# A block-sparse attention with a token and a channel mixer: four chunk pairs by seven block products and one plain chunk, in place of three pairs and three plain chunks

## Chip, cores, metric

One core of a Trainium2 chip. The metric is device time in microseconds of one execution, the median of the runs. Engines are named as in the profile: PE is TensorE, DVE VectorE, ACT ScalarE, POOL GpSimd, SP SyncE.

## What is computed

```python
scores = q @ k.T / sqrt(64), rel = i - j kept where 0 <= rel < 64     # batch 8, heads 8, seq 576, head_dim 64
x = softmax(scores) @ v                          # as (8, 576, 512)
h = relu(x^T @ w_tok1) @ w_tok2                  # 576 -> 256 -> 576 over tokens
u = x + h^T
out = u + relu(u @ w_ch1) @ w_ch2                # 512 -> 1536 -> 512 over channels
```

Weights come as 64-bit floats and are turned into 32-bit ones on the chip. All large products use a pair (hi, lo) for each operand: hi is the operand rounded by a cast, lo the rest, and three matmuls (hi x hi, hi x lo, lo x hi) make one product.

## The kernel before, in words

**Attention** (lines 481 to 594, passes i = -1 to 36). 36 tiles of 128 query rows; each pass works on several tiles at once. In pass i TensorE transposes the exponentials of tile i (`pp`, L312), runs a piece of the second token product (`up`, L413 and L420), the first token product of earlier tiles (`h`, L372), the value product (`xp`, L324), the scores of tile i+2 (`s`, L282) and a second piece of `up`. ScalarE copies `pp` to `pt` (L314), casts a weight piece (`w1hi`, L109), makes eight exponentials per tile in two groups of four (L305), each followed by a reading of the sum, copies `up` to `u` between the groups (L425), casts `xhi` (L109) and copies the second piece of `up`. VectorE makes the masked scores (L297), a reciprocal, the steps of a weight conversion (L204 to L219), and the scaling of `xp` to `x` (L341). GpSimd makes `xlo` (L112), the last add of a conversion (`w`, L221) and `w1lo`. `up` has one PSUM buffer until pass 35. Every engine works through its queue in the order in which the program issues.

**Jobs.** The weights' conversion is cut into 39 jobs of up to 384 columns (0 to 3 and 4 to 6 the token weights, 7 to 22 the first channel weight, 23 to 38 the second). `JOBS` says how many a pass takes; `N_FIRST` = 28 are done in the attention, the other 11 in plain chunk 0.

**Channel mixer.** The 4608 tokens are nine chunks of 512. A *plain* chunk is 144 matmuls into `gp` (`gemm1`, L635), a relu with split (L622, L623), and 144 into `op` (`gemm2`, L643). A *pair* of chunks takes both as the columns of a 2 x 2 block matrix and needs seven block products in place of eight (`first_product`, L913, `second_product`, L969): 12 units of 42 matmuls, 504 in place of 576. The weights' block sums m1 to m7 that pairs need are in DRAM (`w1s`, `w2s`); `load_unit` brings one unit's into a ring of three slots three units ahead. Chunks 0, 1 and 2 are plain (`N_PLAIN` = 3), and three pairs follow. While chunks 1 and 2 run, `weight_steps` forms the sums on VectorE and ScalarE, 128 x 256 at a time, and SyncE stores them; in chunk 2 the first pair's token blocks are combined (`sums`, `prep`).

Of the kernel before, what the change touches and what calls it, by code (L numbers as in the profile page):

```python
# [3 lines left out]

# [17 lines left out]
C = H * D  # L22
# [17 lines left out]
N_FIRST = 28  # L40


JOBS = {i: 1 if 0 <= i < 5 or i in (7, 8, 12, 18, 27) or i > 8 and i % TPP not in (0, 3, 5) else 0 for i in range(-1, 37)}
# [10 lines left out]
N_PLAIN = 3  # L54
# [4 lines left out]
HOME = {"m1": "c2", "m6": "c3", "m7": "c4", "m5": "c5", "m2": "c6", "m4": "c0", "m3": "c1"}  # L59
# [6 lines left out]
STEPS_FT = {1: (2, 2, 2, 2, 1, 0, 2, 2, 0, 1, 1, 0), 2: (2, 1, 0, 1, 1, 0, 0, 0, 0, 0, 0, 0)}  # L66
STEPS_CT = {1: (2, 2), 2: (3, 0)}
# [23 lines left out]
def mixer_kernel(ctx: ExitStack, tc: tile.TileContext, qh, kh, vh, wt1, wt2, wc1, wc2, out):  # L91
# [11 lines left out]
    w1s = [dram.tile([P, NH, NPROD, 2, P], F32, name=f"w1s{k}") for k in range(2)]  # L103
    w2s = [dram.tile([P, NG, 2, NPROD, 2, P], F32, name=f"w2s{k}") for k in range(2)]
# [26 lines left out]
    with ExitStack() as actx:  # L131
# [6 lines left out]
        kbs, loaded, cpool = {}, {}, [pq]  # L138
# [47 lines left out]
        abs_of = {}  # L186

        def job_abs():
            if to_convert:
                n, raw = to_convert[0]  # L190
                m = jobs[n][4]
                abs_of[n] = cpool[0].tile([P, CW], I32, name=f"c{n}", tag="cvc", bufs=2)[:, :m]
                high = raw[:, :m].bitcast(F32).rearrange("p (n t) -> p n t", t=2)[:, :, 1]
                nc.scalar.activation(abs_of[n].bitcast(F32), high, AF.Abs)

        def to_f32_a(raw, n, tag, late=False):
# [3 lines left out]
            if late:  # L200
                c = abs_of.pop(tag)
            else:
                c = cpool[0].tile([P, CW], I32, name=f"c{tag}", tag="cvc", bufs=2)[:, :n]
                nc.vector.tensor_scalar(out=c, in0=high, scalar1=0x7FFFFFFF, scalar2=None, op0=ALU.bitwise_and)  # L204
# [4 lines left out]
            return c, low, high, n, tag, late  # L209

        def to_f32_b(c, low, high, n, tag, late):

            r = cpool[0].tile([P, CW], I32, name=f"r{tag}", tag="cvr", bufs=1)[:, :n]
            w = cpool[0].tile([P, CW], F32, name=f"w{tag}", tag="cvw", bufs=2)[:, :n]
# [6 lines left out]
            (nc.vector if late else nc.gpsimd).tensor_add(w, rf, cf)  # L221
# [5 lines left out]
        jobs += [(wc1, w1hi, w1lo, o, CW) for o in range(0, NCT * F, CW)]  # L227
# [3 lines left out]
        def job_load():  # L231
            if to_load:
                n = to_load.pop(0)
                src, _, _, o, m = jobs[n]
                raw = cpool[0].tile([P, CW], I64, name=f"raw{n}", tag="raw", bufs=3)
                nc.sync.dma_start(raw[:, :m], src[:, o:o + m])
                to_convert.append((n, raw))
# [3 lines left out]
        def job_convert_a():  # L241
            if to_convert:
                n, raw = to_convert.pop(0)
                to_convert_b.append((n, to_f32_a(raw, jobs[n][4], n, n >= N_FIRST)))

# [7 lines left out]
        def job_finish():  # L253
            if to_finish:
# [5 lines left out]
                else:  # L260
                    eng = nc.vector if src is wt2 or n >= N_FIRST else nc.gpsimd
                    split(nc.scalar, eng, hi[:, o:o + m], lo[:, o:o + m], w)
                    if src is wt1 and o + m == 5 * DT:
                        for c, r in enumerate((top, bottom)):
                            nc.gpsimd.tensor_copy(t1z[r, c], t1lo[r, 4 * DT:].bitcast(F32))

# [216 lines left out]
        for i in range(-1, NT + 1):  # L483
# [63 lines left out]
            while to_load and len(to_convert) < 2 and i < NT - 2:  # L547
                job_load()
            if i == NT - 1:
                while to_convert or to_convert_b or to_finish:  # L550
                    job_convert_a()
                    job_convert_b()
                    job_finish()
                qctx.close()
                pu = uctx.enter_context(tc.tile_pool(name="pu", bufs=1, side="right", reuse_waits="tile"))
                ul = {0: load_u(0, pu)}
        for ct in range(NCT):
# [4 lines left out]
    with ExitStack() as bctx:  # L562
# [15 lines left out]
        cpool[0] = pl  # L578
        first = [(o, min(C, jobs[N_FIRST][3] - o)) for o in range(0, jobs[N_FIRST][3], C)]
        w2_raw = []  # L580

        def load_w2():
            if first:
                o, m = first.pop(0)
                raw = pl.tile([P, C], F32, name=f"raww2_{o}", tag="raww2", bufs=2)
                nc.sync.dma_start(raw[:, :m], w2_dram[:, o:o + m])
                w2_raw.append((o, m, raw))

        def split_w2():
            if w2_raw:  # L590
                o, m, raw = w2_raw.pop(0)
                split(nc.scalar, nc.vector, w2hf[:, o:o + m], w2lf[:, o:o + m], raw[:, :m])

        to_load += range(N_FIRST, len(jobs))
        for n in to_load:
            jobs[n] = (wc2, w2hf, w2lf) + jobs[n][3:]
        for _ in range(3):
            job_load()

        def late_steps():  # L600

            job_abs()
            yield
            while to_convert or to_convert_b or to_finish:
                job_convert_a()
                if to_load:
                    job_load()
                yield
                job_finish()
                yield  # L610
                job_convert_b()
                job_abs()
                yield

        late = late_steps()

        def w1_at(ft, ct):
            o = (ft // NH * NCT + ct) * NH * P + ft % NH * P
            return slice(o, o + P)

# [18 lines left out]
        def gemm2(op, ct, fts, gs, first, last, cols=slice(0, CHUNK)):  # L639
            k = 0  # L640
            for ft, (ghi, glo) in zip(fts, gs):
                for w, x in ((w2hi, ghi), (w2hi, glo), (w2lo, ghi)):
                    nc.tensor.matmul(op, w[:, ct, ft], x[:, cols], start=(first and k == 0),  # L643
# [15 lines left out]
        def store_w1(m, k, f0, ct, src):  # L659
# [434 lines left out]
```

## Time and profile before

| | |
|---|---|
| time, median of 3 runs | 805.61 us (805.21 to 806.02) |
| profiled execution | 806.01 us, its span 804.1 us |
| granted TensorE clock | 0.999 |
| attention, to the first `gp` matmul | 255.8 us |
| plain chunks 0, 1, 2 | 66.5, 65.3, 67.0 us |
| three pairs, to the last matmul | 345 us |
| DMA traffic | 180.59 MB, mean 225 GB/s |

Times in the timeline are us from the span's start. A row there gives start, length, engine, line, operation, tiles, and in brackets how long the engine stood idle before it and for whom. Matmuls are pipelined: a 512-column matmul is listed with 0.39 us, but starts follow each other closer. In the windows view, columns are the window, its length, busy time and count of PE, PEld, DVE, ACT and POOL, then the clock, the DMA share and GB/s.

### The profile page before, as it was taken

Reading aid. Unit: us, or ns where it says so; the run is one execution under the profiler, and the core shown is the slowest. Engines: PE = TensorE matmul, PEld = TensorE weight load, DVE = VectorE, ACT = ScalarE, POOL = GpSimd, SP = SyncE. Lnnn points to the kernel's source line nnn. Section 1 sums busy time; section 2 is a strip of 40 time slices with the busy share of each in tenths; the row PEclk is TensorE's granted clock in tenths of the full one; section 3 lists DMA queues with packets and bytes.
Section 4 is the critical chain, followed back from the end, with each engine's and each line's share of the span. In section 5 each row is a group of like instructions: output and inputs, shape, how many; then the busy total and the mean of one; then the engine's idle time right before and its main releaser. Section 6 shows DMA issues by size and latency. Waiting matters only on the chain. (4 is left out here: it accounts for less than half of the span.)

```text
span 804.1 us, 15810 instructions
## 1 busy us (share of the span) xinstructions
PE 789.7 (98%) x5749; PEld 655.2 (81%) x5749; DVE 567.8 (71%) x1529; ACT 388.4 (48%) x1124; POOL 265.1 (33%) x241
## 2 busy tenths in 40 slices
PE   8999999999999999999999999999999999999997
PEld 6667888888889878888878888888888888888886
DVE  5978789589572895777787474756666666656576
ACT  6998889889874440323334141326332244324040
POOL 3634544445330000000000050549832648723140
PEclk9999999999999999999999999999999999999999
DMA  9856778768635637877555775764985755965543
GB/s 352 274 183 227 231 252 302 236 211 297 218 113 169 198 102 213 255 227 236 196 170 179 281 287 183 246 239 170 315 327 206 287 187 166 364 228 190 199 161 104
DMA packets 86828, 180.59 MB, mean 225 GB/s; under 512 B 8800, under 2 KB 51808, under 8 KB 84832
## 3 DMA queue, kind: packets, MB, share of 16 engines
q1 hardware_dynamic: 84640, 177.76, 64.1%
q10 hardware_dynamic: 2112, 1.84, 0.7%
q8 instruction: 45, 0.74, 0.4%
q14 instruction: 31, 0.25, 0.1%
HBM read 137.69 MB, written 41.88 MB: 223 GB/s over the span
## 5 line engine op out<-in xcount | busy, mean ns | idle before, releaser
L913 PE MATMUL gp<-m,w1hi 128*128 128x512 f32 x504 | 155.8, 390 | 0.4 <-POOL m L794 0.4
L112 POOL TENSOR_TENSOR m7lo<-t3g,m7hi 128x512 fp32r<-128x512 f32 x18 | 23.4, 1302 | 359.5 <-ACT m7hi L109 359.5
L305 ACT ACTIVATE e<-e,nm 128x128 f32<-128x128 f32 x288 | 112.3, 399 | 6.1 <-DVE nm L297 6.1
L913 PEld LDWEIGHTS gp<-m,w1hi 128*128 128x128 f32 x504 | 94.7, 188 | 20.9 <-POOL m L794 1.3
L913 PE MATMUL gp<-m,w1lo 128*128 128x512 f32 x252 | 98.2, 389 | 0.0
L958 DVE TENSOR_TENSOR uf<-op,uf 128x512 f32<-128x512 f32 (+1 forms) x91 | 61.9, 684 | 40.5 <-PE op L969 30.7
L297 DVE CUSTOM_DVE_ANT_0 e<-s,mask 128x128 f32<-128x128 f32 x288 | 63.5, 286 | 12.2 <-PE s L282 12.1
L305 ACT ACTIVATION_READ_ACCUMULATOR e<-e,nm 128x1 f32 x288 | 56.5, 196 | 0.0
L112 POOL TENSOR_TENSOR xlo<-x,xhi 128x512 fp32r<-128x512 f32 x32 | 41.2, 1287 | 46.0 <-ACT xhi L109 45.7
L635 PE MATMUL gp<-uhi,w1hi 128*128 128x512 f32 x144 | 56.1, 389 | 0.0
L635 PE MATMUL gp<-ulo,w1hi 128*128 128x512 f32 x144 | 56.1, 389 | 0.0
L635 PE MATMUL gp<-uhi,w1lo 128*128 128x512 f32 x144 | 56.1, 389 | 0.0
L913 PEld LDWEIGHTS gp<-m,w1lo 128*128 128x128 f32 x252 | 47.3, 188 | 9.7
L643 PE MATMUL op<-ghi,w2hi 128*128 128x512 f32 x128 | 50.0, 390 | 0.9 <-ACT ghi L622 0.9
L643 PE MATMUL op<-glo,w2hi 128*128 128x512 f32 x128 | 50.0, 390 | 0.2 <-DVE glo L623 0.2
L643 PE MATMUL op<-ghi,w2lo 128*128 128x512 f32 x128 | 49.9, 389 | 0.0
L916 ACT COPY x<-gp 128x512 f32<-128x512 f32 x18 | 10.6, 587 | 81.2 <-PE gp L913 81.2
L221 POOL TENSOR_TENSOR w<-r,c 128x384 f32<-128x384 f32 (+1 forms) x28 | 27.6, 985 | 60.5 <-DVE r L219 58.5
L324 PEld LDWEIGHTS xp<-v,pt 128*64 128x64 f32 x1152 | 36.6, 138 | 12.9 <-ACT e L305 10.1
L341 DVE TENSOR_TENSOR x<-xp,ri 128x512 f32<-128x512 f32 x36 | 24.8, 690 | 30.3 <-PE xp L324 29.7
L312 PE MATMUL pp<-ident,e 128*128 128x128 f32 x288 | 44.6, 281 | 1.4
L420 PE MATMUL up<-t2hi,hhi 128*128 128x320 f32 (+1 forms) x128 | 43.0, 336 | 0.0
(204 smaller groups left out, 2042.4 us busy)
## 6 DMA issues: line engine op xcount, KB each, us to landing
v<-vh SPq DMA_DIRECT2D x36, 512.0 KB, 3.8
w1hi<-w1s SPq DMA_DIRECT2D x18, 896.0 KB, 4.9
w1lo<-w1s SPq DMA_DIRECT2D x18, 896.0 KB, 6.9
w1hi<-w2s SPq DMA_DIRECT2D x18, 896.0 KB, 4.6
w1lo<-w2s SPq DMA_DIRECT2D x18, 896.0 KB, 6.4
raw<-wc SPq DMA_DIRECT2D x32, 384.0 KB, 4.4
q<-qh SPq DMA_DIRECT2D x36, 256.0 KB, 4.9
k<-kh SPq DMA_DIRECT2D x7, 1280.0 KB, 8.3
```

The costliest lines, as they stand in the source:

```text
L112: eng_lo.tensor_sub(lo, src, hi.bitcast(F32))
L221: (nc.vector if late else nc.gpsimd).tensor_add(w, rf, cf)
L297: nc.vector.tensor_tensor_reduce(out=e[:, h], in0=s[:, h], in1=mk, scale=-scale, scalar=MAX_F32, op0=ALU.add, op1=ALU.min, accum_out=nm[:, ...
L305: nc.scalar.activation(e[:, h], e[:, h], AF.Exp, bias=nm[:, g:g + 1], scale=-1.0, accum_out=sm[:, g:g + 1])
L312: nc.tensor.transpose(pp[:, h], e[:, h], ident)
L324: nc.tensor.matmul(xp[half * BLK:(half + 1) * BLK, h], pts[h % 2][:, h // 2, half * BLK:(half + 1) * BLK], vt[:, half, h], start=True, sto ...
L341: nc.vector.tensor_mul(x, xp, ri.unsqueeze(2).to_broadcast([P, H, D]))
L420: nc.tensor.matmul(up[:, :n], hx[:, cs], w[:, tt * S + s0:tt * S + s0 + n], start=False, stop=(k == 6), skip_group_check=True)
L635: nc.tensor.matmul(gp, w[:, w1_at(ft, ct)], x[:, ct], start=(k == 0), stop=(k == 3 * NCT - 1))
L643: nc.tensor.matmul(op, w[:, ct, ft], x[:, cols], start=(first and k == 0), stop=(last and k == 3 * len(gs) - 1), skip_group_check=not (fir ...
L913: nc.tensor.matmul(b[INTO[m]], w[:, at], c[:, h, t], start=(k < 4 and z == y == 0), stop=(z == 1 and y == 2), skip_group_check=True)
L958: eng.tensor_add(x, y, x)
```

## The change

`N_PLAIN` is 1: chunk 0 alone is plain, and eight chunks make four pairs.

- 35 of the 39 conversion jobs now lie in the attention (`JOBS`: one more in passes 21, 30, 32 and two in passes 31, 33, 34 and 35); the last four run in chunk 0 (`tail_job`), through `w2_dram`.
- The first channel weight's sums are formed in the attention, passes 15 to 34 (`sums1_steps`). One block goes through five steps: VectorE adds hi and lo back together; GpSimd makes four sums; ScalarE casts the first row's hi and issues its store; GpSimd makes its lo, ScalarE casts the second row's hi and issues its store; GpSimd makes that lo. The lo stores are issued by ScalarE at the next step. `shi`, the cast's tile, has one buffer. Raw blocks are stored by SyncE (`RAW1`).
- The second weight's sums: two of six blocks in chunk 0, four in the first pair (`SUMS2`), GpSimd and ScalarE again. The first pair's token blocks are combined in chunk 0.

```diff
-N_FIRST = 28
+N_FIRST = 35
-N_PLAIN = 3
+N_PLAIN = 1
+SUMS1 = {i: (1, 0) for i in (15, 17, 18, 21, 25, 28)}
+SUMS1.update({i: (1, 1) for i in (16, 19, 20, 22, 24, 26, 27, 29, 30, 31, 33, 34)})
...
+        def store_sums():
+            for to, t in sum_stores:
+                nc.scalar.dma_start(to.rearrange("p m x -> p (m x)"), t.bitcast(F32))
+            sum_stores.clear()
+
+        def sum_steps(whole, buffers, negate, target, one_row):
+
+            w = buffers(None)
+            whole(w)
+            yield
+            (a11, a12), (a21, a22) = ([x[:, c * WW:(c + 1) * WW] for c in range(2)] for x in w)
+            nc.gpsimd.tensor_add(a22, a22, a21)
+            nc.gpsimd.tensor_sub(a21, a11, a21)
+            nc.gpsimd.tensor_sub(a11, a22, a11)
+            nc.gpsimd.tensor_sub(a12, a12, a11)
+            yield
+            for rows in ((0,), (1,)) if one_row else ((0, 1),):
+                his = [buffers(r) for r in rows]
+                for r, hi in zip(rows, his):
+                    if negate and r == 1:
+                        nc.scalar.mul(a22, a22, -1.0)
+                    nc.scalar.copy(hi, w[r])
+                    nc.scalar.dma_start(target(0, 2 + 2 * r).rearrange("p m x -> p (m x)"), hi.bitcast(F32))
+                yield
+                for r, hi in zip(rows, his):
+                    lo = w[r].bitcast(F32R)
+                    nc.gpsimd.tensor_sub(lo, w[r], hi.bitcast(F32))
+                    sum_stores.append((target(1, 2 + 2 * r), lo))
+                if rows[-1] == 1 or not one_row:
+                    yield
...
+                    return pq.tile([P, C], F32R, name=f"shi{f}_{r}", tag="shi", bufs=1)
...
             if i >= N_START:
                 for _ in range(n_jobs):
                     job_convert_b()
+            sums1_steps(SUMS1.get(i, (0, 0))[0])
+            for _ in range(RAW1.get(i, 0)):
+                next(raw1_left)
...
+            sums1_steps(SUMS1.get(i, (0, 0))[1])
```

ScalarE's queue in pass 20, before, from one `pt` to the next (the digits behind a name are the tile's or job's number and a buffer number):

```order
L314 COPY pt20_1_2502<-pp20_1_2497 128x512
L109 CAST w1hi_66<-w15_2425 128x384
L305 ACTIVATE e21_0_2506,sum21_2505<-e21_0_2506,nm21_2504 128x128 x4
L425 COPY u2_1_2481<-up2_1_1_2525 128x320
L305 ACTIVATE e21_1_2511,sum21_2505<-e21_1_2511,nm21_2504 128x128 x4
L109 CAST xhi20_2593<-x20_2573 128x512
L425 COPY u2_1_2481<-up2_1_2_2597 128x320
L314 COPY pt21_0_2619<-pp21_0_2614 128x512
```

The same place now, `shi1_0` and `shi1_1` being the two rows' casts of block 1 and `w1s0` the DRAM tensor that takes them:

```order
L390 COPY pt20_1_2528<-pp20_1_2523 128x512
L115 CAST w1hi_66<-w15_2442 128x384
L381 ACTIVATE e21_0_2532,sum21_2531<-e21_0_2532,nm21_2530 128x128 x4
L501 COPY u2_1_2503<-up2_1_1_2551 128x320
L381 ACTIVATE e21_1_2537,sum21_2531<-e21_1_2537,nm21_2530 128x128 x4
L298 CAST shi1_0_2582<-sw1_0_2448 128x512
L299 DMA w1s0_69<-shi1_0_2582 128x512
L115 CAST xhi20_2622<-x20_2602 128x512
L501 COPY u2_1_2503<-up2_1_2_2626 128x320
L298 CAST shi1_1_2640<-sw1_1_2449 128x512
L299 DMA w1s0_69<-shi1_1_2640 128x512
L390 COPY pt21_0_2652<-pp21_0_2647 128x512
```

Two casts and two stores stand between the exponentials and the next `pt`. GpSimd's queue at the same place, before:

```order
L112 TENSOR_TENSOR w1lo_67<-w15_2425,w1hi_66 128x384
L221 TENSOR_TENSOR w16_2551<-r16_2550,c16_2536 128x384
L112 TENSOR_TENSOR xlo20_2594<-x20_2573,xhi20_2593 128x512
L112 TENSOR_TENSOR w1lo_67<-w16_2551,w1hi_66 128x384
L112 TENSOR_TENSOR xlo21_2708<-x21_2687,xhi21_2707 128x512
```

And now, L303 being the low part of a block's row, which reads `shi`:

```order
L118 TENSOR_TENSOR w1lo_67<-w15_2442,w1hi_66 128x384
L216 TENSOR_TENSOR w16_2577<-r16_2576,c16_2562 128x384
L118 TENSOR_TENSOR xlo20_2623<-x20_2602,xhi20_2622 128x512
L303 TENSOR_TENSOR sw1_0_2448<-sw1_0_2448,shi1_0_2582 128x512
L118 TENSOR_TENSOR w1lo_67<-w16_2577,w1hi_66 128x384
L216 TENSOR_TENSOR w17_2708<-r17_2707,c17_2693 128x384
L303 TENSOR_TENSOR sw1_1_2449<-sw1_1_2449,shi1_1_2640 128x512
```

The first row's low part stands behind `xlo20`, the second's behind `w17`. GpSimd's queue in passes 32 to 34, before:

```order
L112 TENSOR_TENSOR xlo32_4067<-x32_4042,xhi32_4066 128x512
L221 TENSOR_TENSOR w25_4137<-r25_4136,c25_4116 128x384
L112 TENSOR_TENSOR xlo33_4180<-x33_4159,xhi33_4179 128x512
L221 TENSOR_TENSOR w26_4257<-r26_4256,c26_4242 128x384
L112 TENSOR_TENSOR xlo34_4282<-x34_4279,xhi34_4281 128x512
```

And now, with block 5's four sums (L288 to L291):

```order
L118 TENSOR_TENSOR xlo32_4220<-x32_4195,xhi32_4219 128x512
L216 TENSOR_TENSOR w29_4297<-r29_4296,c29_4272 128x384
L216 TENSOR_TENSOR w30_4303<-r30_4302,c30_4276 128x384
L288 TENSOR_TENSOR sw5_1_4099<-sw5_1_4099 128x256
L289 TENSOR_TENSOR sw5_1_4099<-sw5_0_4098,sw5_1_4099 128x256
L290 TENSOR_TENSOR sw5_0_4098<-sw5_1_4099,sw5_0_4098 128x256
L291 TENSOR_TENSOR sw5_0_4098<-sw5_0_4098 128x256
L118 TENSOR_TENSOR xlo33_4352<-x33_4331,xhi33_4351 128x512
L216 TENSOR_TENSOR w31_4439<-r31_4438,c31_4420 128x384
L216 TENSOR_TENSOR w32_4445<-r32_4444,c32_4424 128x384
L303 TENSOR_TENSOR sw5_0_4098<-sw5_0_4098,shi5_0_4370 128x512
L118 TENSOR_TENSOR xlo34_4476<-x34_4473,xhi34_4475 128x512
```

The four sums stand behind the adds of two jobs (`w29`, `w30`), and the low part behind two more.

More of the change, by code (lines that the diff above doesn't have):

```diff
@@ L753, in load_unit, with sums2, whole @@
+        def sums2(n, buffers):
+            g, t = divmod(n, 2)
+            def whole(w):
+                for row in range(2):
+                    o = ((2 * row + t) * NFT + 4 * g) * P
+                    nc.sync.dma_start(w[row], w2_dram[:, o:o + 2 * WW])
+            return sum_steps(whole, buffers, True, lambda k, at: w2s[k][:, g, t, at:at + 2], False)
         def load_unit(n):
```

394 lines of the change are left out of this document (187 added, 207 removed).

## The prediction

> **What bounds the kernel now.** I read the page first, then TensorE's timeline at the stage borders, then the chain of waits.
>
> ```profile
> span 804.1 us, 15810 instructions
> ...
> PE 789.7 (98%) x5749; PEld 655.2 (81%) x5749; DVE 567.8 (71%) x1529; ACT 388.4 (48%) x1124; POOL 265.1 (33%) x241
> ...
> ACT  6998889889874440323334141326332244324040
> POOL 3634544445330000000000050549832648723140
> ```
> TensorE is busy throughout. ScalarE is at eight or nine tenths in the first third, which is the attention, and at a third after it.
>
> ```profile
> 255.82 0.39 PE L635 MATMUL gp<-uhi,w1hi 128*128 128x512 f32 x1
> ...
> 322.30 0.39 PE L635 MATMUL gp<-uhi,w1hi 128*128 128x512 f32 x1
> ...
> 454.57 0.62 PE L913 MATMUL gp<-m,w1hi 128*128 128x512 f32 x2
> ```
> These rows of the timeline are the first matmuls of plain chunk 0, of plain chunk 1, and of the first pair. So the attention takes 255.8 us, plain chunk 0 66.5, and plain chunks 1 and 2 together 132.27.
>
> ```profile
> 531.10 19.05 PE gp L913 x84
> ...
> 761.37 19.04 PE gp L913 x84
> ```
> In the chain, the same place of the first and of the third pair lies 230.27 us apart: one pair takes 115.13 us, borders included. From 19.04 us for 84 matmuls, a 512-column matmul takes 0.2267 us. Plain chunks and pairs are TensorE's, with hardly a wait.
>
> In the attention, one tile as an example (tile 25), ScalarE and then TensorE:
>
> ```profile
> 170.85 1.07 ACT L314 COPY pt<-pp 128x512 f32<-128x512 f32 x2
> ...
> 175.25 0.39 ACT L305 ACTIVATE e<-e,nm 128x128 f32<-128x128 f32 x1
> ...
> 175.64 0.62 ACT L109 CAST xhi<-x 128x512 fp32r<-128x512 f32 x1
> 177.02 0.37 ACT L425 COPY u<-up 128x256 f32<-128x256 f32 x1 [0.77 <-PE up L420]
> 177.51 1.07 ACT L314 COPY pt<-pp 128x512 f32<-128x512 f32 x2
> ```
> ```profile
> 175.83 0.44 PE L413 MATMUL up<-ident,x 128*128 128x128 f32 x2
> ...
> 176.82 1.03 PE L312 MATMUL pp<-ident,e 128*128 128x128 f32 x8
> 177.69 0.38 PE L413 MATMUL up<-ident,x 128*128 128x128 f32 x2
> ...
> 180.11 1.15 PE L324 MATMUL xp<-v,pt 128*64 128x64 f32 x32
> 181.19 1.10 PE L282 MATMUL s<-k,q 64*64 64x128 f32 x32
> 182.23 0.44 PE L413 MATMUL up<-ident,x 128*128 128x128 f32 x2
> ```
> A tile takes 6.66 us (170.85 to 177.51). TensorE issues without a pause; ScalarE has 0.77 us to spare, just ahead of its second copy of `up`. TensorE needs that copy at 177.69 and `pt` at 180.11: a ScalarE that is late by more than these margins stops it, since `up` has one buffer.
>
> **The change part by part.** The sum is made against the profiled execution, 806.0 us (span 804.1), 0.4 above the median of the runs, 805.6.
>
> *Matmuls.* A pair has 504 matmuls, two plain chunks 576. Plain chunks 1 and 2 go (132.27 us) and a fourth pair comes (115.13): **-17.1 us**. Of that 72 x 0.2267 = 16.3 is arithmetic; the rest is a wait of plain chunk 2, less a pair's border. If the new chunk 0 has that wait too, it is 16.3: small.
>
> *Weight sums in the attention.* For each of six blocks VectorE adds hi and lo twice (512 columns, 0.69 us as in the row below), GpSimd makes four sums of 256 columns and two low parts, and ScalarE makes two casts and issues four stores.
>
> ```profile
> 234.49 0.69 DVE L341 TENSOR_TENSOR x<-xp,ri 128x512 f32<-128x512 f32 x1 [0.89 <-PE xp L324]
> ...
> L221 POOL TENSOR_TENSOR w<-r,c 128x384 f32<-128x384 f32 x17 | 17.1, 1003 | 35.0 <-DVE r L219 33.0 <-issue 2.0
> L112 POOL TENSOR_TENSOR xlo<-x,xhi 128x512 fp32r<-128x512 f32 x19 | 24.5, 1290 | 31.2 <-ACT xhi L109 31.2
> ...
> L769 SPq DMA_DIRECT2D r<-u_dram x28: 319/430/653, 392.4 to 633.6; - x28
> ...
> 252.86 0.62 ACT L109 CAST uhi<-uf 128x512 fp32r<-128x512 f32 x1 [1.28 <-issue]
> ```
> GpSimd: 1.29 us for 512 columns and 1.00 for 384, so an estimated 0.71 for 256. A DMA issued by ScalarE holds it: two of them stand behind the 1.28 "issue". A 256 KB issue is taken at SyncE's median, 0.43. ScalarE gains 12 casts of 0.55 (spacing of the casts) and 24 issues of 0.43: 16.9 us over some 20 tiles of 6.66. At 0.77 us to spare per tile that is 15.4: on average it would just fit, if it fell evenly. It doesn't.
>
> In tiles 20, 24, 27 and 30 both casts of a block fall into one tile, and they share one buffer (`shi`, one copy). The second cast waits for GpSimd's low part of the first, and that stands in GpSimd's queue behind `xlo`, which waits for ScalarE's `xhi`. Walked on tile 25's rows: exp ends 175.64; first cast to 176.19, its issue to 176.62, `xhi` to 177.17, the copy of `up` to 177.54 (in time for 177.69). GpSimd: `xlo` 177.2 to 178.5, low part to 179.8. Second cast to 180.35, issue to 180.8, first `pt` half at 181.3 in place of 178.0. Queued behind the waiting cast are both `pt`, all eight exponentials and the next `up`. TensorE's `xp` starts at 181.35 in place of 180.11: 1.2 us. Then `pt`, `w1hi`, four exponentials and the copy end at 184.15, where TensorE wants `up` at 183.45: 0.75. Then four more, a store, `xhi` and the copy end at 187.05; TensorE wants it at 186.05: 1.05. Sum 3.0, then ScalarE has caught up. Tile 30 has no `w1hi` cast: 2.6. Tile 24 has slack of its own:
>
> ```profile
> 168.70 0.62 ACT L109 CAST xhi<-x 128x512 fp32r<-128x512 f32 x1 [1.25 <-DVE x L341]
> 170.36 0.43 ACT L425 COPY u<-up 128x320 f32<-128x320 f32 x1 [1.04 <-PE up L420]
> ```
> There the waits of 1.25 and 1.04 us hide the first cast and its issue, and I keep 1.3. The first block has its casts a tile apart: two thirds of a double, 2.0.
>
> The last block is in tiles 33 and 34, where VectorE also gets two conversions per tile:
>
> ```profile
> 224.94 0.31 DVE L204 TENSOR_SCALAR c<-raw 128x384 int32<-128x384 int32 x1
> ...
> 227.13 0.56 DVE L219 SCALAR_TENSOR_TENSOR r<-raw,r 128x384 f32<-128x384 uint32 x1
> ...
> 230.70 1.07 ACT L314 COPY pt<-pp 128x512 f32<-128x512 f32 x2
> ...
> 233.29 1.15 PE L324 MATMUL xp<-v,pt 128*64 128x64 f32 x32
> ```
> One conversion is 2.75 us (224.94 to 227.69); two end at 230.4. Then GpSimd adds `w30` (to 231.5) and makes the four sums (to 234.3); only then ScalarE may cast (234.9) and issue (235.3). `pt` comes at 235.9 in place of 231.2, `xp` stands 2.6 us from 233.29. The next four exponentials then end at 238.0 (236.4 + 1.6), about 0.8 after TensorE wants the last of them: 3.4.
>
> Attention: 2.0 + 3.0 + 1.3 + 3.0 + 2.6 + 3.4 = **+15.3 us**. Lower bound 3: each block costs only what its casts and issues exceed the spare time by. Upper bound 24: 9 more, as the third rival has it.
>
> *Stores.* SyncE gets 24 stores of raw blocks ahead of `v`, `q` and the load of chunk 0:
>
> ```profile
> SPq L155 <- PE xp L324: 106.9, 24, 6.2
> ...
> 204.17:235.80 31.63, 31.57 (x437) 27.53 (x435) 21.40 (x104) 27.92 (x107) 9.55 (x9) 1.00 0.57 184
> ```
> SyncE stands 106.9 us waiting for `v` buffers, and the DMA share in these tiles is 0.57: cost 0, bound 0 to 1 where `uf` of chunk 0 is late.
>
> *Plain chunk 0.* Within 144 first products (32.6 us) VectorE gets four conversions (11 us), twelve `glo`, and twelve sums and low parts of 512 columns (24 x 0.69): 27.6 us. TensorE is covered while VectorE is no more than the four PSUM banks behind; bound 0 to 3, taken 0.
>
> *First pair.* Four blocks of the second weight's sums, each 4 x 0.71 + 2 x 1.29 = 5.4 us on GpSimd, in 115 us that hold 24 low parts of 1.29. Loads come two units (19 us) ahead. Bound 0 to 5, taken 0.
>
> Sum: -17.1 + 15.3 = **-1.8**: 804.2 for the profiled execution, **803.8** beside the median.
>
> **Rivals.**
>
> *Spare time absorbs it (796).* If the casts and issues use what ScalarE has spare, attention grows by 7 instead of 15.3. For: the 0.77 us. Against: the queue orders above.
>
> *VectorE becomes the bound in tiles 30 to 34 (811).* They get five more conversions and two whole adds: 5 x 2.75 + 1.4 = 15.1 us. In 204.17 to 235.80 VectorE is busy 21.40 of 31.63, so 10.2 is free: 4.9 too much, and up to 4.5 more if the waits for `xp` (0.89 in tile 34) can't be filled. Middle 7.1 on top: 803.8 + 7.1 = 810.9. It decides as soon as TensorE's own stops leave VectorE less than 5 us there. Against: the stop of 3.4 gives some back.
>
> *VectorE and GpSimd hold each other up (813).*
>
> ```profile
> L218 DVE TENSOR_SCALAR r<-c x22: 359/360/991, 59.9 to 238.2; 128x384 int32<-128x384 int32 x22
> ```
> The same instruction takes 0.36 or, beside a running GpSimd add, 0.99. GpSimd gets 12 low parts, 24 sums and 7 adds in the attention; each that catches one such instruction costs 0.63, 27 us in all, of which at most a third can lie on the path: +9, 812.8. The Trainium skill (SBUF — State Buffer, Who interferes with whom) says that GpSimd and a VectorE instruction in a two-port mode exclude each other for a whole instruction, and this row agrees; by that rule alone every overlap would count and the sum would be 27 higher, 831. The trace speaks against that: the median is 0.36.
>
> *GpSimd late in the first pair (808).* +5 if the sums push `m4lo` past its use.
>
> **How the numbers follow.** The measurement tells about 0.2%, 1.6 us. The forecast has 0.42 (0.23 faster, 0.14 same, 0.05 slower, since its 799 to 807 straddles the line), the first rival 0.27, VectorE's 0.18, the hold-up 0.07, the first pair 0.06. Faster 0.50, same 0.14, slower 0.36. Range 793.5 (attention +5) to 813.
>
> **What would show it.** Right: first `gp` of chunk 0 at about 271; ScalarE waiting for GpSimd at L298 by 2 us in tiles 20, 24, 27, 30 and 4 in 33; TensorE's waits in the attention naming `pt` and `up`; chunk 0 near 66.5 and four pairs near 115. Wrong: attention under 262 (the spare time was real) or over 275; or a first pair over 118.

## The result

The changed kernel took 841.96 us (median of 4 runs, 839.53 to 843.68) against 805.62 (805.21 to 806.02): a ratio of 1.0449, interval 1.0422 to 1.0476. It is slower, by 36.3 us, where 803.8 was forecast and 813 was the end of the range.

### The profile page after: what moved, and what is told of

Its sections match the earlier page's. It is cut to its first block, busy times and chain, and to the rows that moved or that the text cites. A ratio compares the mean times of both kernels' runs of the same rounds, so it can differ in the third digit from the quotient of the medians.

```text
span 839.7 us, 15754 instructions
## 1 busy us (share of the span) xinstructions
PE 786.2 (94%) x5677; PEld 645.7 (77%) x5677; DVE 584.3 (70%) x1448; ACT 401.4 (48%) x1130; POOL 423.2 (50%) x384
## 4 chain that ended last, share of the span: by engine, by line
PE 45%; POOL 10%; DMA 5%; issue 3%; ACT 2%; DVE 1%; SPq 1%; ACTq 0%; DVEq 0%; POOLq 0%
PE gp L917 21%; PE op L973 20%; POOL m L801 5%; PE op L716 3%; POOL uf L962 2%; DMA u_dram<-u 2%; DMA w1lo<-w2s 1%; DMA raww<-w_dram 1%; POOL w2lo L118 1%; POOL m4lo L118 1%; DMA out<-uf 0%; PE gp L708 0%; SPq L757 0%; POOL m6lo L118 0%; POOL m7lo L118 0%
## 5 line engine op out<-in xcount | busy, mean ns | idle before, releaser
L917 PE MATMUL gp<-m,w1hi 128*128 128x512 f32 x672 | 208.2, 390 | 3.3 <-DVE x L926 2.5
L917 PEld LDWEIGHTS gp<-m,w1hi 128*128 128x128 f32 x672 | 126.1, 188 | 31.8 <-DVE x L926 2.9
L917 PE MATMUL gp<-m,w1lo 128*128 128x512 f32 x336 | 130.8, 389 | 0.0
L962 DVE TENSOR_TENSOR uf<-op,uf 128x512 f32<-128x512 f32 (+1 forms) x121 | 82.5, 685 | 55.7 <-PE op L973 40.9
L400 PE MATMUL xp<-v,pt 128*64 128x64 f32 x1152 | 44.1, 233 | 9.4 <-ACT pt L390 9.2
L358 PE MATMUL s<-k,q 64*64 64x128 f32 x1152 | 42.3, 283 | 1.9 <-DMA k<-kh 1.4
L489 PE MATMUL up<-ident,x 128*128 128x128 f32 x144 | 28.6, 289 | 13.8 <-ACT u L501 13.7
L962 DVE TENSOR_TENSOR u<-op,u 128x512 f32<-128x512 f32 x40 | 27.4, 684 | 19.0 <-PE op L973 17.0
L390 ACT COPY pt<-pp 128x512 f32<-128x512 f32 x72 | 39.0, 588 | 3.2 <-ACT shi L298 2.4
L388 PEld LDWEIGHTS pp<-ident,e 128*128 128x128 f32 x288 | 33.6, 142 | 8.8 <-ACT e L381 7.4
```

Of the source, the lines that this page charges most:

```text
L358: nc.tensor.matmul(so, qt[r, j, half], kbs[b][r, n:n + 2, j], start=True, stop=True)
L388: nc.tensor.transpose(pp[:, h], e[:, h], ident)
L390: nc.scalar.copy(pt, pp)
L400: nc.tensor.matmul(xp[half * BLK:(half + 1) * BLK, h], pts[h % 2][:, h // 2, half * BLK:(half + 1) * BLK], vt[:, half, h], start=True, sto ...
L917: nc.tensor.matmul(b[INTO[m]], w[:, at], c[:, h, t], start=(k < 4 and z == y == 0), stop=(z == 1 and y == 2), skip_group_check=True)
L962: eng.tensor_add(x, y, x)
```

## The profile after

Its profiled execution took 841.5 us. From the page: span, busy times, and two of the engines' rows in 40 slices.

```profile
span 839.7 us, 15754 instructions
...
PE 786.2 (94%) x5677; PEld 645.7 (77%) x5677; DVE 584.3 (70%) x1448; ACT 401.4 (48%) x1130; POOL 423.2 (50%) x384
...
PE   8989988798977997989899999999999999999997
...
DVE  5978799979888458427375766666674857666666
```

TensorE, busy throughout before, now has holes in the first 20 slices of 21 us, which reach into the first pair; after them it is as before. TensorE's timeline at the borders of the stages:

```profile
292.43 0.39 PE L708 MATMUL gp<-uhi,w1hi 128*128 128x512 f32 x1
...
367.55 0.62 PE L917 MATMUL gp<-m,w1hi 128*128 128x512 f32 x2
...
489.50 0.62 PE L917 MATMUL gp<-m,w1hi 128*128 128x512 f32 x2
```

| stage | before, us | after, us | change | forecast |
|---|---|---|---|---|
| attention (to the first gp) | 255.8 | 292.4 | +36.6 | +15.3 |
| plain chunk 0 | 66.5 | 75.1 | +8.6 | 0 |
| two plain chunks out, one pair in | 132.3 | 115.1 | -17.2 | -17.1 |
| first pair | 114.6 | 121.9 | +7.4 | 0 |

The sum is +35.4; the two spans are 35.6 apart. The trade is as forecast. All three places into which the weight work went cost more.

TensorE over the whole attention, before and after (windows view):

```profile
0.00:255.82 255.82, 248.30 (x3370) 210.37 (x3371) 193.59 (x869) 214.21 (x795) 107.85 (x117) 1.00 0.70 238
```
```profile
0.00:292.43 292.43, 256.57 (x3371) 214.51 (x3371) 238.50 (x922) 218.78 (x806) 150.08 (x160) 0.98 0.77 260
```

It stands idle for 35.9 us instead of 7.5, and it is busy for 8.3 us longer with the same matmuls. The second part has to do with its clock, which stays at 1.00 before and here drops to 0.50 for 3.4 us from 211.1, 3.4 us from 238.4 and 6.8 us from 262.3. The first of these stretches, and the 3.4 us ahead of it:

```profile
207.65:211.05 3.40, 0.76 (x4) 0.28 (x2) 2.81 (x8) 1.00 (x2) 0.17 (x1) 1.00 0.54 184
211.07:214.47 3.40, 3.17 (x56) 3.05 (x60) 0.69 (x1) 3.40 (x15) 2.18 (x3) 0.50 0.35 119
```

A matmul into `xp`, 222 ns in the median, takes 317 ns in that stretch. TensorE is busy for 12.1 of the 13.7 us at half clock, so they cost an estimated 6 us at most (half of 12.1). Each of the three begins right after 3.4 us in which TensorE stood idle for 2.0 us or more (2.66, 3.29 and 2.03). In every trace here the clock changes at multiples of 3.41 us from one another. Cut into pieces of that length, the stretch of 40 to 500 us shows the same in all kernels: a piece at full clock that half clock follows holds at least 1.69 us of idle time, one that full clock follows at most 1.87. So a long enough stop of TensorE is paid a second time, and the forecast has no term for that.

What TensorE and ScalarE waited for in the attention, 100 to 280 us (total in us, times, longest):

```profile
ACT xhi L115 <- DVE x L417: 22.0, 11, 4.2
...
PE up L489 <- ACT u L501: 13.7, 15, 1.9
...
ACT shi L298 <- DMA w1s<-shi: 11.6, 3, 5.5
...
PE xp L400 <- ACT pt L390: 9.2, 4, 4.6
ACT shi L298 <- POOL sw L303: 6.0, 3, 3.3
...
ACT shi L298 <- POOL sw L291: 5.2, 2, 2.7
...
PE h L448 <- POOL xlo L118: 4.7, 2, 2.6
```

On its face this is the forecast: TensorE waits for `up` and `pt` (and for `xlo`, which the forecast didn't have), ScalarE's casts at L298 wait for GpSimd (11.2 us), and for something else that it didn't have, the landing of the first cast's own store out of the single `shi` buffer (11.6 us). But the longest row is another: `xhi` waits 22.0 us for VectorE. VectorE in tile 30, and GpSimd beside it:

```profile
224.57 0.43 DVE L411 SCALAR_TENSOR_TENSOR ri<-sum 128x8 f32<-128x8 f32 x1
...
225.16 0.74 DVE L198 TENSOR_SCALAR c<-raw 128x384 int32<-128x384 int32 x1
225.93 0.78 DVE L200 TENSOR_SCALAR c<-c 128x384 f32<-128x384 f32 x1
226.74 0.78 DVE L201 TENSOR_SCALAR c<-c 128x384 int32<-128x384 int32 x1
...
229.50 0.68 DVE L417 TENSOR_TENSOR x<-xp,ri 128x512 f32<-128x512 f32 x1
```
```profile
224.94 0.74 POOL L288 TENSOR_TENSOR sw<-sw 128x256 f32<-128x256 f32 x1
225.75 0.74 POOL L289 TENSOR_TENSOR sw<-sw,sw 128x256 f32<-128x256 f32 x1
226.57 0.73 POOL L290 TENSOR_TENSOR sw<-sw,sw 128x256 f32<-128x256 f32 x1
```

The three VectorE instructions of 0.31 to 0.36 us take 0.74 to 0.78, each about as long as the GpSimd sum beside it, as if the two engines took turns. `x`, whose operand `xp` lies in PSUM, keeps its 0.68. So there are two theories. **A:** ScalarE's in-order queue, as forecast. **B:** VectorE, by the amount of its work (B2) and by GpSimd's work beside it (B1); **C** is B2's part that the late conversions make (the forecast's second rival).

## The experiments

All stages are from the profiled execution of each kernel (us); medians and ratios against the kernel before on the same chip. "Half clock" is how many us of the attention ran at a granted clock of 0.50; they cost at most half of that. A stage is one execution's: profiled executions lie up to 4.4 us from their kernel's median (e2: 823.0 against 818.7), and at tile 14, ahead of the sums, e2 is already 0.7 us late and e10 1.5 early. A difference of 2 or 3 us between two stages is therefore not settled.

| run | attention | half clock | chunk 0 | first pair | median | ratio, interval |
|---|---|---|---|---|---|---|
| after | 292.4 | 13.7 | 75.1 | 121.9 | 842.0 | 1.0449, 1.0422 to 1.0476 |
| e1 | 288.6 | 13.7 | 75.7 | 121.7 | 837.6 | 1.0401, 1.0376 to 1.0426 |
| e2 | 270.4 | 13.7 | 77.5 | 122.8 | 818.7 | 1.0167, 1.0128 to 1.0206 |
| e3 | 283.7 | 13.7 | 76.6 | 123.7 | 832.4 | 1.0342, 1.0314 to 1.0370 |
| e4 | 288.2 | 13.7 | 74.7 | 122.3 | 839.7 | 1.0425, 1.0393 to 1.0457 |
| e5 | 292.6 | 17.1 | 67.8 | 126.2 | 840.2 | 1.0432, 1.0403 to 1.0460 |
| e6 | 293.1 | 20.5 | 76.9 | 120.8 | 841.3 | 1.0442, 1.0416 to 1.0467 |
| e7 | 295.6 | 20.5 | 75.1 | 118.6 | 837.5 | 1.0405, 1.0375 to 1.0434 |
| e8 | 293.7 | 23.9 | 73.8 | 123.9 | 842.3 | 1.0449, 1.0423 to 1.0474 |
| e9 | 273.0 | 10.2 | 77.3 | 120.3 | 823.0 | 1.0226, 1.0200 to 1.0252 |
| e10 | 278.7 | 17.1 | 76.9 | 121.4 | 828.8 | 1.0294, 1.0279 to 1.0309 |
| e11 | 267.4 | 6.8 | 75.5 | 122.5 | 815.8 | 1.0138, 1.0116 to 1.0161 |
| e12 | 287.7 | 17.1 | 67.8 | 118.8 | 826.5 | 1.0270, 1.0255 to 1.0285 |
| e13 | 275.2 | 6.8 | 67.1 | 117.3 | 813.9 | 1.0104, 1.0087 to 1.0121 |
| e14 | 276.9 | 13.7 | 67.6 | 117.5 | 813.5 | 1.0100, 1.0083 to 1.0117 |
| e15 | 271.2 | 0 | 67.1 | 120.2 | 807.4 | 1.0029, 1.0017 to 1.0042 |
| e16 | 272.0 | 3.4 | 67.9 | 117.9 | 808.5 | 1.0038, 1.0026 to 1.0050 |
| e17 | 264.5 | 0 | 66.2 | 120.8 | 803.6 | 0.9977, 0.9963 to 0.9991 |
| e18 | 254.8 | 0 | 66.7 | 114.6 | 804.9 | 1.0002, 0.9994 to 1.0011 |

### The attention: ScalarE's waits (e1)

The edit, shortened, as are those further down:

```diff
-tag="shi", bufs=1
+tag="shi", bufs=2
-name=f"q{i}", tag="q", bufs=5
+name=f"q{i}", tag="q", bufs=4
```

> The cast block of the sums gets two buffers (shi), and q has four buffers instead of five to make room. Theory A (the second cast of a block waits for the landing of the first cast's own store, and ScalarE's copies of pt and up stand behind it): ScalarE's 11.6 us of waits for that store go, its 11.2 us of waits for GpSimd stay, first gp of plain chunk 0 near 279 instead of 292.4, total near 829. Theory B (VectorE is held up by GpSimd's adds, or has too many conversions): the waits only change their name, first gp at 289 or later, total 838 or more. Plain chunk 0 and the first pair stay at 75 and 122.

The waits for the store are gone, and with them only 3.8 us of the attention. `up` waits for ScalarE 15.8 us instead of 13.7, and `xhi` for VectorE 27.3 instead of 22.0: most of it changed its name. Theory A's number, 279, is missed by 10; theory B's (289 or later, 838 or more) by less than 1.

### Leaving parts out (e2, e3, e4)

> The first weight's block sums are left out of the attention: no adds on VectorE, no sums or low parts on GpSimd, no casts and no stores by ScalarE; SyncE stores raw words in their places (12 stores of 512 KB), so the four middle products of the first weight are not formed. The seven added conversions stay. Theory A and theory B for GpSimd's adds: first gp near 257, total near 806. Theory C (the seven conversions overfill VectorE in tiles 30 to 34): first gp stays at 264 or later, total 814 or more.

> The seven conversions of the second weight that were moved into the attention (jobs 28 to 34) are left out: their raw words are loaded and a finished piece of the first weight is stored in their place, so the second weight is not formed. The sums stay. Theory A: first gp 3 to 6 us earlier than 292.4, since the last block's cast no longer stands behind GpSimd's add of a conversion, total 836 to 839. Theory C: first gp 10 us or more earlier, total 831 or less.

> The four sums of 256 columns per block on GpSimd (24 in the attention) are left out; the casts, low parts and stores stay, so the middle products of the first weight get wrong weights. Theory A: only ScalarE's 5.2 us of waits for these sums go, first gp near 287, total near 836. Theory B (24 sums of 0.735 us, 17.6 us in all, hold VectorE up): VectorE's 0.36 us instructions keep their length, first gp at 280 or earlier, total 829 or less.

Without any sums the attention is 22.0 us shorter, but still 14.6 longer than before: theory C was right about a part. Against the tiles of the kernel before, the start of `pt` is level from tile 14 to 31 (0.69 us late in both) and 11.1 late at the last `pt`, in tile 35: tiles 31 to 35, with two conversions in each of four, cost 10.4 us. TensorE was at half clock for 6.8 us there and busy for 4.7 of them, which can make up 2.4 of the 10.4. (The last 3.5 come after; that they come from `uf`, which lands behind this run's twelve big stores, is not tested.) Without the conversions the sums cost 27.9, and the attention is 8.7 shorter, between the two forecasts. Leaving out the 24 sums alone brings 4.2 (2.3 by the medians, whose intervals overlap), less than theory A expected and far less than B.

### ScalarE freed of the sums (e8)

```diff
-nc.scalar.copy(hi, w[r])
-nc.scalar.dma_start(target(0, 2 + 2 * r), hi)
+nc.gpsimd.tensor_copy(hi, w[r])
+sum_stores.append((target(0, 2 + 2 * r), hi))   # issued by nc.sync
```

> The first weight's block sums stay in the attention with all their results, but ScalarE does nothing for them: GpSimd makes the 12 casts ahead of its low parts, and SyncE issues the 24 stores, a step after each result; shi has two buffers (q four). Theory A (ScalarE's in-order queue is what the sums cost, 22 us): first gp near 272 instead of 292.4, as without the sums (270.4), total near 821. Theory B (GpSimd's work beside VectorE is what they cost): first gp at 283 or later, total 832 or more, with VectorE's 0.36 us instructions stretched.

This speaks against theory A: ScalarE does nothing for the sums, and the attention is no shorter (293.7, against 288.6 in e1, which has two `shi` buffers too; 10.2 us more at half clock can account for 3 of the difference). But GpSimd gets twelve casts more here; e11 below puts ScalarE's part back alone. ScalarE's waits in 100 to 285 us:

```profile
ACT xhi L115 <- DVE x L421: 44.9, 17, 6.6
```

It now waits 44.9 us for VectorE: most of the time that the casts and stores took, ScalarE now spends waiting.

### Each engine's part alone (e9, e10, e11)

Each puts one engine's part back into the kernel without sums: VectorE's twelve `nc.vector.tensor_add(w[row], ...)`; GpSimd's L288 to L291 and L303 on two fixed tiles; ScalarE's L298, L299 and L279 from fixed tiles.

> As without the first weight's sums (first gp at 270.4), but VectorE's twelve adds are back at their places; nobody reads them. The middle products of the first weight are still raw words. Theory B2 (it is the sum of VectorE's work that is too much, each added us counts once the spare time is gone): first gp 4 to 8 us later than 270.4. Theory B1 (what costs is GpSimd's work beside VectorE): 3 or less.

> As without the first weight's sums (first gp at 270.4), but GpSimd's 24 sums and 12 low parts are back at their places, on two fixed tiles of zeros, so that nobody waits for them and they wait for nobody. Theory B1 (exclusive use between GpSimd and VectorE's instructions with two operands in SBUF): first gp 9 us or more later than 270.4, with VectorE busy about 11 us longer for the same instructions. Theory B2: 3 or less.

> As without the first weight's sums (first gp at 270.4), but ScalarE's 12 casts and 24 stores are back at their places, from fixed tiles and with two buffers, so that they wait for nobody; SyncE's 12 big stores, which stood for them, go. Theory B: first gp within 4 us of 270.4. Theory A: 10 us or more later (12 x 0.55 + 24 x 0.33 = 14.5 us of ScalarE's time).

From tile 14 to tile 31, `pt` falls behind the kernel before by 5.1 us with VectorE's adds, 6.9 with GpSimd's operations, 2.9 with ScalarE's part, 0.0 with none and 27.6 in the changed kernel. The first `gp` comes 2.6 later than without sums, 8.3 later and 2.9 earlier (ScalarE's run has no big stores by SyncE). Counted from tile 14 on, so that the kernels' different starts drop out, it comes 4.6 later, 10.5 later and 1.6 earlier. So ScalarE's part is small, as theory B had it. GpSimd's is the largest, near B1's 9, though 3 of it can be half clock. VectorE's fits B1 (3 or less) by the first count and B2 (4 to 8) by the second, so it doesn't decide.

GpSimd's part costs in two ways. One was in neither theory: nobody reads the results of the added operations in e10, but GpSimd's own `xlo` stands behind them in its queue, as here behind four sums (L343 to L346):

```profile
243.68 0.73 POOL L343 TENSOR_TENSOR fixed<-fixed 128x256 f32<-128x256 f32 x1
...
246.79 1.38 POOL L118 TENSOR_TENSOR xlo<-x,xhi 128x512 fp32r<-128x512 f32 x1
```
```profile
248.22 0.80 PE L466 MATMUL h<-xlo,t1hi 128*128 128x512 f32 x1 [2.57 <-POOL xlo L118]
```

In five places TensorE waits for such an `xlo`, 4.3 us in all; without sums it never does. In the changed kernel two of its waits, 4.7 us, are for an `xlo` behind a block's four sums. The other way is VectorE: its same instructions are longer, 17.9 us in all over the attention (227.95 against 210.02 us busy, 909 instructions in both). No run separates the two. VectorE's groups at 100 to 250 us (busy, mean ns), without sums and then with GpSimd's operations alone:

```profile
L417 DVE TENSOR_TENSOR x<-xp,ri 128x512 f32<-128x512 f32 x21 | 14.5, 689 | 11.5 <-PE xp L400 11.5
L200 DVE TENSOR_SCALAR c<-c 128x384 f32<-128x384 f32 x23 | 9.8, 427 | 0.8
...
L198 DVE TENSOR_SCALAR c<-raw 128x384 int32<-128x384 int32 x23 | 8.7, 377 | 3.1 <-DMA raw<-wc 3.1
```
```profile
L198 DVE TENSOR_SCALAR c<-raw 128x384 int32<-128x384 int32 x22 | 16.7, 761 | 0.0
L200 DVE TENSOR_SCALAR c<-c 128x384 f32<-128x384 f32 x22 | 15.1, 688 | 0.8
L435 DVE TENSOR_TENSOR x<-xp,ri 128x512 f32<-128x512 f32 x19 | 13.0, 686 | 6.0 <-PE xp L418 6.0
```

The conversions' first step doubles (377 to 761 ns); `x`, which reads PSUM, doesn't move. The Trainium skill (SBUF — State Buffer, Who interferes with whom) says that a VectorE instruction in a two-port mode, or with both inputs in SBUF, contends with GpSimd's reads, and one with at most one input in SBUF outside those modes does not. The row of `x`, with one input in SBUF, agrees with the second half; those of L198 and L200 agree with the first if they run in such a mode, which no view here shows.

Why the parts add to 14.9 alone and to 27.6 together is seen in part in VectorE's total. Each row: stretch, its length, then busy time of PE, PEld, DVE, ACT, POOL; from 100 us to 4.7 us ahead of the first `gp`, before and after:

```profile
100.00:251.12 151.12, 150.28 (x2013) 132.51 (x2011) 115.45 (x498) 126.67 (x467) 61.23 (x53) 1.00 0.69 232
```
```profile
100.00:287.70 187.70, 159.06 (x2007) 136.65 (x2006) 160.65 (x552) 131.62 (x475) 103.52 (x96) 0.96 0.78 259
```

VectorE was idle for 35.7 us there and got 45.2 more: 7 x 2.75 + 12 x 0.69 = 27.5 of work and 17.7 of being held up. As long as a part fits the idle time, most of it is free; the parts together don't fit. But this sum alone, 9.5 too much, doesn't give the 36.6: 27.1 us of idle time are left, since VectorE also has to wait for others in it (9.2 us for `xp`), and work that comes at another place can't use it. Another share, 9.5 us up to tile 31, is the single `shi` buffer (18.1 with two), though all but 3.8 of it was lost again by the end. What each share costs when all come together is not separated.

### Plain chunk 0 (e5, e6)

ScalarE, VectorE and TensorE in plain chunk 0 of the changed kernel:

```profile
304.18 0.62 ACT L115 CAST w2hi<-raww 128x512 fp32r<-128x512 f32 x1 [8.21 <-DMA raww<-w_dram]
```
```profile
305.33 0.69 DVE L696 SCALAR_TENSOR_TENSOR glo<-gp,ghi 128x512 fp32r<-128x512 f32 x1 [5.93 <-ACT ghi L695]
...
310.10 1.34 DVE L200 TENSOR_SCALAR job<-job 128x384 f32<-128x384 f32 x1
```
```profile
319.68 0.50 PE L708 MATMUL gp<-uhi,w1hi 128*128 128x512 f32 x1 [2.58 <-DVE glo L696]
```

The first cast of a second-weight piece waits 8.21 us for its load, with `ghi` behind it; VectorE stands 5.93 us for `ghi`, is then behind, and one of its instructions takes 1.34 us in place of 0.36. The two edits: the splits begin at ft 3 instead of 0 (e5); all `w2lo` on VectorE (e6).

> The splits of the second weight in plain chunk 0 begin after its fourth product instead of its first (ft 3 to 11), so that no cast of a piece that is still on its way stands between ScalarE's ghi. Theory D (chunk 0 lost 8.7 us because VectorE stood 5.9 us behind ScalarE's 8.2 us wait for the first raww): chunk 0 falls from 75.1 to 70 or less, total near 837. Theory E (VectorE is slowed there by GpSimd's w2lo): chunk 0 stays at 73 or more. The attention stays at 292, the first pair at 122.

> The six low parts w2lo that GpSimd makes in plain chunk 0 go to VectorE, at their places. Theory E: VectorE's 0.36 us instructions there keep their length and about 7 us of stretching go, against 6 x 0.69 = 4.1 us of added work: chunk 0 near 72. Theory D or a plain excess of VectorE work: chunk 0 at 77 or more (+2 to +4).

The later splits bring chunk 0 from 75.1 to 67.8, nearly the 66.5 of before, with GpSimd's `w2lo` in place: the waiting cast was the cause. (The changed kernel has 3.4 us at half clock in this stage, but e1 has none and takes 75.7.) Theory E falls: without GpSimd's part the chunk is no shorter (76.9, with 6.8 us at half clock). Of e5's 7.3 us the first pair took 4.2 back (126.2): TensorE waits 4.99 us instead of 2.50 for `x`, which waits for the landing of the raw blocks' stores, and is at half clock for 6.8 us there. So the median fell by 1.8 only, to 840.2, where 837 was expected.

### The first pair (e7) and the three mends together (e12)

TensorE's two longest waits there, and ScalarE just ahead of them:

```profile
375.64 0.74 PE L917 MATMUL gp<-m,w1hi 128*128 128x512 f32 x2 [2.50 <-DVE x L926]
...
407.26 0.50 PE L973 MATMUL op<-m2hi,w1hi 128*128 128x512 f32 x1 [2.24 <-ACT u L980]
```
```profile
373.43 0.59 ACT L920 COPY x<-gp 128x512 f32<-128x512 f32 x1 [21.10 <-DMA w2s<-w2lo]
...
404.14 0.62 ACT L298 CAST wt<-wr 128x512 fp32r<-128x512 f32 x1 [4.80 <-POOL wr L291]
```

`x` lies where `w2lo` was and waits until the last store out of it has landed; later a cast of a block's sums waits 4.80 us for GpSimd with the copy of `u` behind it.

The edit; block 5's casts move in the same way:

```diff
-            store_raw2(ct)
+            if ct < 2:
+                store_raw2(2 * ct)
+                store_raw2(2 * ct + 1)
...
-(2, "m3"): (3,), (3, "m1"): (3, 4), (3, "m3"): (4,)
+(3, "m1"): (3,), (3, "m7"): (3,), (3, "m5"): (4,), (3, "m3"): (4,)
```

> Two orders are changed, the work is the same: the stores of the second weight's raw blocks are issued in the first two quarters of plain chunk 0's second products instead of one in each quarter, and the casts of blocks 3 and 5 in the first pair are issued one product later. Theory F (the first pair waits 2.5 us because x lies where w2lo was and that one's last store lands late, and 2.2 and 1.4 us because u and m2hi stand on ScalarE behind casts that wait for GpSimd's sums): the first pair falls from 121.95 to 116 to 117.5, total near 836.5. Rival: GpSimd itself is too slow there, and the waits move to m4lo or m6lo: 120 or more. Attention and chunk 0 stay.

> The whole computation, with three edits at once: two shi buffers, the later splits in plain chunk 0, the changed orders at the end of chunk 0 and in the first pair. If they add up: attention 288.6, chunk 0 67.8, first pair 118.6, total 841.5 - 3.8 - 7.3 - 3.4 = 827. If the first pair waits for the late stores of the raw blocks once chunk 0 is shorter (126.15 with the later splits alone), 831 or more. Slower than before in any case.

All three waits are gone in e7, a new one of 2.27 us (`x` again, behind the next block's cast, with 3.4 us at half clock after it) has come: 118.6, a little over what was expected. The attention of that run is 3.1 longer, in a stage that the edit doesn't touch: it has 6.8 us more at half clock. The changed kernel's own four runs, 839.5 to 843.7, also come in the order of their granted clocks, 0.992 to 0.979. The three mends add up as worked out (826.5, expected 827): 15.4 of the 36.3 us.

### Taking work from VectorE (e13 to e18)

With the mends in, e13 converts in pieces of 512 columns (28 conversions instead of 35) and forms the sums on the converted pieces, without VectorE's adds, in tiles 11 to 25; `q` and the raw pieces have fewer buffers. e14 also moves one cast in the first pair. e15 interleaves the two weights' pieces, which spreads the blocks over tiles 11 to 34. e16 gives the sums' stores to SyncE. e17 is e15 without this instruction from tile 7 on:

```diff
-nc.vector.scalar_tensor_tensor(out=ri, in0=sm, scalar=1e-9, in1=sm, op0=ALU.add, op1=ALU.max)
-nc.vector.reciprocal(ri, ri)
+nc.vector.reciprocal(ri, sm)
```

e18 is the kernel before with the same leaving-out.

> The whole computation, with the three mends, and the attention's weight work cut for VectorE: both large weights are converted in pieces of 512 columns instead of 384 (28 conversions in the attention instead of 35, at most one per tile), and the block sums are made on the converted pieces themselves, so VectorE's twelve adds go. ScalarE's casts and stores and GpSimd's sums and low parts are all still there, in tiles 11 to 25. Theory B2+C (the attention is longer because VectorE has more work than it has time for): VectorE's added work falls from 7 x 2.75 + 12 x 0.69 = 27.5 us to about 21 x 0.5 = 10.5, attention 262 to 270 instead of 287.7, total 801 to 809, about as before. Theory B1 (GpSimd's work beside VectorE is what costs): attention 276 or more, total 815 or more. Theory A (ScalarE): 280 or more.

> As the kernel with wide pieces, and in the first pair the cast and the low part of block 4 come two products later. The first pair falls from 118.8 to 117 if x stood behind that cast; it stays if GpSimd's queue is what is late. Attention and chunk 0 as in the kernel with wide pieces.

> As the kernel with wide pieces, where all 18.8 us of the attention's loss came in tiles 13 to 25, in which the six blocks followed each other every two to three tiles; the pieces of the second weight now come between those of the first, so that the blocks are spread over tiles 11 to 34. Work and shapes are the same. Theory A2 (with VectorE relieved it is ScalarE that is overfull where blocks crowd: 2 casts of 0.55, 4 stores of 0.33 and 2 more casts for the pieces in two tiles with 0.77 us to spare in each): attention 262 to 268 instead of 275.2, total 801 to 807. Theory B1 (every operation of GpSimd beside VectorE costs, wherever it is): 273 or more, total 812 or more.

> As the kernel with spread blocks, and SyncE issues the 24 stores of the sums instead of ScalarE. Theory A2: another 24 x 0.33 = 7.9 us come off ScalarE, attention 257 to 263, total 796 to 802, faster than before. Rival: the stores stand on SyncE behind loads of v, which wait 6.2 us for a buffer, and GpSimd or ScalarE wait for them: no better than with spread blocks alone.

> As the kernel with spread blocks, but from tile 7 on VectorE no longer adds 1e-9 to the sums of the exponentials before the reciprocal (128 x 8 elements, median 0.44 us and up to 1.10 in that kernel, once in a tile); the sums are at least 1, where float32 doesn't feel that addend. Nothing else changes. Theory B2 (VectorE is what the attention's last 15 us wait for): about 22 x 0.4 = 9 us of VectorE's time go, attention 262 to 266 instead of 271.2, total 798 to 802, faster than before. Theory A2 (ScalarE alone): 270 or more, total 806 or more.

> The kernel before, with the same leaving-out and no other change. There VectorE has 36.5 us to spare in tiles 14 to 36, so nothing should change: attention 255.8, total 804.5 to 806. If it gains as much as the kernel with spread blocks, the gain is not one of the new kernel's.

e13 takes 12.5 us off the attention of e12, with all of ScalarE's casts and stores and of GpSimd's sums kept; up to 4.4 of it go with the half clock. From tile 31 to the last `pt` it loses nothing, where the kernel without sums lost 10.4: theory C's part is gone. The rest, 18.6 us in tiles 13 to 25, leaves it at 275.2, between B2's numbers (262 to 270) and B1's (276 or more). Spreading the blocks brings 4.1 (271.2, short of 262 to 268), and up to 3 of that is the half clock, of which e15's attention has none; e14 and e16 bring nothing, so neither the issue of stores nor that cast is what is waited for. In the changed kernel the chain of waits can be followed back only to 277.8 us, so it says nothing of the attention's middle; in e15 it runs through, and its row by engines, over the whole span, names VectorE second:

```profile
PE 53%; DVE 23%; POOL 11%; issue 4%; ACT 4%; DMA 3%; SPq 1%; DVEq 0%; ACTq 0%; POOLq 0%
```

From 100 us to the first `gp`, VectorE holds 115 of the chain's 171 us in e15, and 61 of 164 in e17.

The last pair of runs is the cleanest. VectorE in e15 and in e17, over the same stretch as above:

```profile
100.00:266.40 166.40, 155.49 (x2069) 134.24 (x2064) 143.69 (x500) 132.93 (x482) 95.84 (x83) 1.00 0.86 292
```
```profile
100.00:259.75 159.75, 152.50 (x2008) 131.90 (x2007) 135.84 (x477) 130.66 (x471) 97.22 (x81) 1.00 0.88 300
```

One 128x8 instruction per tile goes, VectorE is busy 7.9 us less, and the attention is 6.7 us shorter, both at full clock. Not all of it is the edit's: 1.1 us of it lie ahead of tile 7, where the edit begins, and the medians are 3.8 apart. The kernel before, with the same edit, stays: 804.9, ratio 1.0002 (0.9994 to 1.0011). There VectorE was idle for 35.7 of 151 us, in e15 for 22.7 of 166. e17, at 803.6 (12 runs), is faster than both kernels, by 0.23% than before (interval 0.09% to 0.37%); the 798 to 802 expected of it are missed.

## Why the prediction was wrong

- *The trade, -17.1:* right, -17.2.
- *The attention, +15.3:* wrong by 21.3. The places were right: the tiles in which TensorE stops are the ones named, and it stops for `up` and `pt`. The step that failed is the accounting of "spare time": it was made for ScalarE only ("0.77 us to spare"). VectorE's two adds of each block got a duration and no place, the added conversions and GpSimd's hold-up were put among the rivals. The runs show the reverse: with ScalarE freed nothing was gained (e8), its part alone cost 2.9 up to tile 31 and nothing up to the first `gp` (e11), and the time follows VectorE's (e13, e17). Two more terms were missing: TensorE at half clock after its stops, an estimated 6 us at most, and `xlo` behind the blocks' sums in GpSimd's queue, 4.7 us of TensorE's waits. The queue walk itself had a flaw too: the second cast waits for the landing of the first cast's store (up to 5.5 us) as well as for GpSimd; that was worth 3.8 (e1).
- *The rivals* were priced as alternatives with chances of 0.18 and 0.07. They were both borne out, and they load the same engine: 10.4 us from the conversions in tiles 31 to 35 (e2; priced 7.1; up to 2.4 of it half clock) and 17.7 us of held-up VectorE time (priced at 27, with a third on the path). "At most a third" assumed that VectorE has slack; what of the 17.7 lies on the path once the slack is used up was not measured by itself. Forecast and rivals summed are 15.3 + 7.1 + 9 = 31.4, against 36.6; that this comes near is luck, since the 15.3 stand for ScalarE's queue, of which e1 found 3.8.
- *Spare time absorbs it (796):* false.
- *Stores of raw blocks, 0:* right for the first weight, where none was shown to cost; for the second weight's, issued in chunk 0, the landing cost 2.5 in the first pair.
- *Plain chunk 0, 0 (0 to 3):* 8.6. The step "27.6 us of VectorE fit into 32.6" held only if VectorE starts on time. It looked at VectorE's amount and not at what stands ahead of `ghi` on ScalarE: a cast that waits for a load (e5).
- *First pair, 0 (0 to 5):* 7.4. GpSimd was not late for the matmuls, as the rival had it; ScalarE's casts waited for GpSimd with `u` behind them, and a reused buffer waited for a store (e7).
- The signs named for a wrong forecast appeared: the attention is over 275, the first pair over 118.

## What to carry to other kernels

When work is moved into a stage that one engine bounds, add up what every engine gets there against what each has to spare, and add the rivals that load the same engine instead of choosing among them. Work put on GpSimd is not free for VectorE: as an upper bound, price each VectorE instruction with its operands in SBUF as if it ran after the GpSimd instruction beside it, and look at what stands behind the new work in GpSimd's own queue. Read the granted clock by windows: a stop of TensorE can cost its length and then half clock. An in-order engine that waits for a load or for a store's landing costs what is queued behind it, so look for that before its busy time.

## What the runs showed of the hardware

- VectorE's `TENSOR_SCALAR` of 128x384 in SBUF took 0.36 us (median) and up to 1.39 beside GpSimd; a 128x512 add of two SBUF tiles 0.68 to 1.50; a 128x8 instruction 0.16 to 1.26. Instructions of 512 columns with an operand in PSUM kept their length (0.675 to 0.692).
- A store of 256 KB issued by ScalarE held it for 0.33 us (priced 0.43); those of the casts landed in a median of 3.9 us. A single buffer behind such a store made the next cast wait up to 5.5 us.
- GpSimd took 0.73 to 0.74 us for an add of 256 columns, as estimated (0.71).
- TensorE's granted clock changed in steps of 3.41 us. After a step at 1.00 with 1.9 us or more of idle time the next one was at 0.50, after one with 1.6 us or less at 1.00 (all kernels here, 40 to 500 us); an `xp` matmul took 317 ns in place of 222 at 0.50.
